# Opening attention with q ahead of k and cosine products on GpSimd, and sending routing logits to all partitions through DRAM

## The chip, the cores and the metric

One core of one Trainium2 chip runs the whole program. The metric is the device time of one execution in microseconds (us). Five engines work side by side, each on its own queue of instructions: TensorE (PE), VectorE (DVE), ScalarE (ACT), GpSimd (POOL) and SyncE (SP, which issues DMAs here; ACT and POOL issue some too).

## The reference

Attention, then two mixtures of experts on its output. Cut to what is computed:

```python
q_rot, k_rot = rotate(q), rotate(k)               # B=2, H=8, S=576, D=64; cos and sin of position
attn = softmax(q_rot @ k_rot.T / sqrt(D)) @ v     # 16 heads
x = attn.transpose(0, 2, 1, 3).reshape(1152, 512)
# first mixture: 8 experts on all tokens, weighted by a Sinkhorn-normalised gate
x = sum(P[:, e:e+1] * (relu(x @ w1[e]) @ w2[e]) for e in range(8))
# second mixture: greedy routing with a capacity of 144 tokens per expert
for idx in argsort(-(x @ w_gate).flatten()):
    tok, e = idx // 8, idx % 8
    if assigned[tok] < 0 and counts[e] < 144:
        assigned[tok] = e; counts[e] += 1
out[assigned == e] = relu(x[assigned == e] @ w1[e]) @ w2[e]
```

## The kernel before, in words

**Opening.** The 16 heads are worked as 8 pairs. Pair 0 has nothing to hide behind, so `attention` writes its first steps out by hand. k of head 0 is loaded first on SP, q of head 0 and the table of cosines and sines (`tcs`) on ACT (L1276 to L1281). The function `first` (L1328) rotates one head on DVE: two products with the sine (L1334, L1335) into a scratch tile `t`, the product with the cosine in place (L1337), and their sum into `t1k` or `t1q` (L1338). It is called for k of head 0, q of head 0 and k of head 1. ACT writes q a second time beside itself (`twice`, L1343). PE transposes both (`tq`, L1382), ACT and DVE copy the transposes out of PSUM as `qk` (L1398, L1400), and PE makes the scores `S` (`sc`, L1415), of which DVE takes the maximum (`mx`, L1424) and ACT the exponential (`ex`, L1429). q of head 1 and all later heads are rotated on GpSimd (`rot`, L1323 to L1326) from wider tables `tabk` and `tabq`, which ACT makes from `tcs`. `warm` (L1375) issues matmuls whose result nobody reads; their numbers are in `WARM`. The order of the steps of one pair is the string `ORDER`; pair 0 follows `FIRST`, the same string with the three steps of head 1's transposes (`tq1 qb1 qa1`) moved behind `te1 pb0 ex2`.

**Routing of the second mixture.** The function `moe2` assigns tokens in 8 phases, one expert filled in each. Phase p takes every token's best logit `m` among the experts still open (`prefer`, L205 and L206), spreads all 1152 values of `m` to all 128 partitions as `mb`, compares them with each partition's own nine (DVE: `compare`, L245 to L248; ACT for the first part of tables j = 5 to 8: `above`, L237 and L239), counts by 81 small matmuls how many tokens stand ahead (`count`, L256), assigns and closes an expert. From that come the token indices (`place`, `spread`, `index`, `address`), two indirect DMAs on GpSimd that gather the tokens (`gather`, L360: `xa`, `xb`), and eight DMAs of 512 KB on SP with the expert's weights (`weights`, L380 and L384). The expert itself is 64 matmuls on 144 tokens (L471, L481) with transposes in and out. Phase 0's `mb`, and that of all others before the change, is made by nine transposes of a broadcast column on PE (`bcast`, L213) and three copies on ACT (`bcopy`, L216).

The order of all this is fixed when the program is built. The class `Plan` holds each step with what it depends on and its booked times, one (engine, duration, latency) for each engine it passes, and always takes the step that can start first. The experts' matmuls are a main line in their own order; routing steps are put between them where the books say that their operands are there:

```python
op(f"bc{c}", ["m"], [("PE", 0.33, 0.2)], bcast, c)
op(f"mb{c}", [f"bc{c}"], [("ACT", 0.37, 0.1)], bcopy, c)
op("wlo", ["sel" if last else "close"] + ...,
   [("SP", 0.3, 0), ("DMA", 7.0 if p else 3.5, 2.0)], weights, 0, 4 if p else 2)
```

`wlo` and `whi` are the two halves of an expert's weight loads. `HOLD` names phases in which DVE waits for the gather of the phase before (`hold`, L335) ahead of compare j.

## Time and profile before

| | |
|---|---|
| time, median of 3 runs | 1123.04 us (1122.49 to 1125.29) |
| the profiled execution's own time | 1122.86 us |
| its span | 1121.1 us, 20946 instructions |
| mean granted clock of TensorE | 0.996 of full speed |
| busy share of the span | PE 98%, DVE 67%, POOL 39%, ACT 37% |
| chain that ended last, by engine | PE 88%, DVE 3%, DMA 3%, issue 2%, ACT 2%, POOL 1% |

The span is what the profiler recorded on the core; the 1.76 us that the execution took beyond it lie before the first and behind the last recorded instruction. The chain of waits is followed back from the last instruction to what released it, so its shares tell on which engine time would have to be saved. In a timeline, each row has its start and its duration in us, the engine, the program line, the operation with output and inputs, and in brackets the idle time before it and what ended that.

### The profile page before, as it was taken

What the parts mean: (1) busy time and instruction counts of PE and PEld (TensorE: products, weight loads), DVE (VectorE), ACT (ScalarE), POOL (GpSimd) and SP (SyncE); (2) the same over time, 40 slices, a digit from 0 to 9 for tenths busy, and PEclk for the clock granted to TensorE, in tenths of its full rate; (3) what the DMA queues carried; (4) which work ended last, traced back from release to release, by engine and by line L of the source; (5) the groups of instructions that cost most, each with busy time, mean ns of one, the idle gap of its engine ahead of it and who ended that gap; (6) DMA issues with size and microseconds to landing.
All of it is one profiled execution on the core that took longest, in us unless ns stands there. A gap on an engine that the chain in (4) does not pass through costs nothing.

```text
span 1121.1 us, 20946 instructions
## 1 busy us (share of the span) xinstructions
PE 1102.6 (98%) x8171; PEld 962.0 (86%) x8171; DVE 745.7 (67%) x1688; ACT 412.8 (37%) x903; POOL 438.6 (39%) x449
## 2 busy tenths in 40 slices
PE   7999999999999999999999999999999999999997
PEld 4666678998888888888888889989889888999997
DVE  5777733564777777777777777666678887778200
ACT  5777742143223223222223223232331133566222
POOL 6778353065434335434334534345310000234211
PEclk8999999999999999999999999999999999999999
DMA  5332322001233222432322422112130004879920
GB/s 130 79 74 51 99 82 76 1 1 57 82 98 94 85 86 88 125 98 75 95 85 75 126 92 66 38 39 74 39 141 11 30 1 165 277 250 354 292 75 22
DMA packets 105458, 107.22 MB, mean 96 GB/s; under 512 B 35600, under 2 KB 68752, under 8 KB 105232
## 3 DMA queue, kind: packets, MB, share of 16 engines
q1 hardware_dynamic: 102528, 100.40, 28.6%
q0 software_dynamic: 2048, 4.72, 1.4%
q8 instruction: 64, 1.05, 0.4%
q10 hardware_dynamic: 784, 0.77, 0.2%
q14 instruction: 34, 0.28, 0.1%
HBM read 98.85 MB, written 4.72 MB: 92 GB/s over the span
## 4 chain that ended last, share of the span: by engine, by line
PE 88%; DVE 3%; DMA 3%; issue 2%; ACT 2%; POOL 1%; SPq 1%; POOLq 0%; DVEq 0%; ACTq 0%
PE Y L1001 23%; PE T L939 21%; PE T L750 9%; PE Y L769 8%; PE Y L471 5%; PE Y L481 5%; PE T L1454 3%; PE S L1415 3%; PE T L1382 3%; DMA fr<-in_moe_w 2%; PE T L256 1%; DVE acc L1003 1%; PE PV L1382 1%; DVE v L952 1%; PE PV L1454 1%
## 5 line engine op out<-in xcount | busy, mean ns | idle before, releaser
L939 PE MATMUL T<-xH,wa 128*128 128x256 f32 (+1 forms) x576 | 137.8, 294 | 0.9 <-ACT v L959 0.8
L939 PEld LDWEIGHTS T<-big,wb 128*128 128x128 f32 x864 | 125.7, 188 | 10.8 <-DVE v L952 1.8
L939 PE MATMUL T<-big,wb 128*128 128x256 f32 (+1 forms) x864 | 133.0, 296 | 0.0
L952 DVE TENSOR_TENSOR v<-T,v 128x256 f32<-128x256 f32 (+1 forms) x240 | 108.1, 450 | 37.4 <-PE T L939 34.5
L1003 DVE SCALAR_TENSOR_TENSOR acc<-Y,pw,acc 128x512 f32<-128x512 f32 x168 | 122.5, 742 | 1.5 <-PE Y L1001 0.4
L939 PEld LDWEIGHTS T<-xH,wa 128*128 128x128 f32 x576 | 100.0, 188 | 9.5 <-ACT v L959 3.8
L750 PE MATMUL T<-xH,wa 128*128 128x384 f32 x336 | 92.9, 337 | 0.0
L848 POOL TENSOR_TENSOR wa<-wraw,wa 128x512 fp32r<-128x512 f32 (+1 forms) x48 | 48.8, 1018 | 106.3 <-ACT wa L847 106.3
L945 ACT ACTIVATE hhA<-v 128x256 fp32r<-128x256 f32 x72 | 30.1, 418 | 149.3 <-DVE v L952 149.3
L939 PE MATMUL T<-xL,wa 128*128 128x256 f32 (+1 forms) x288 | 84.5, 293 | 0.0
L945 ACT ACTIVATE hhB<-v 128x320 fp32r<-128x320 f32 x72 | 34.0, 472 | 136.5 <-DVE v L952 136.5
L946 DVE SCALAR_TENSOR_TENSOR hlB<-v,hhB 128x320 fp32r<-128x320 f32 x72 | 57.0, 792 | 38.7 <-ACT hhB L945 38.7
L1001 PE MATMUL Y<-wa,hhB 128*128 128x512 f32 x240 | 75.2, 395 | 0.0
L1001 PE MATMUL Y<-wb,hhB 128*128 128x512 f32 x240 | 75.2, 395 | 0.0
L1073 DVE SCALAR_TENSOR_TENSOR fr<-fr,fc 128x512 f32<-128x512 f32 x64 | 52.5, 820 | 33.6 <-DMA fr<-in_moe_w 33.6
L946 DVE SCALAR_TENSOR_TENSOR hlA<-v,hhA 128x256 fp32r<-128x256 f32 x72 | 51.1, 709 | 35.3 <-ACT hhA L945 35.3
L867 POOL TENSOR_TENSOR wb<-wraw,wb 128x512 fp32r<-128x512 f32 x24 | 30.6, 1299 | 101.9 <-ACT wb L866 101.9
L867 POOL TENSOR_TENSOR wa<-wraw,wa 128x512 fp32r<-128x512 f32 x24 | 30.6, 1294 | 99.1 <-ACT wa L866 99.1
L769 PE MATMUL Y<-wb,hh 128*128 128x512 f32 x216 | 68.4, 398 | 0.0
L750 PEld LDWEIGHTS T<-xH,wa 128*128 128x128 f32 x336 | 61.3, 188 | 2.9 <-issue 0.9
L1424 DVE TENSOR_REDUCE negmax<-S 128x1 f32<-128x576 f32 x72 | 53.8, 748 | 15.0 <-PE S L1415 14.1
L1001 PE MATMUL Y<-wa,hhA 128*128 128x512 f32 x192 | 59.9, 393 | 0.0
(343 smaller groups left out, 2729.1 us busy)
## 6 DMA issues: line engine op xcount, KB each, us to landing
wraw<-in_moe_w SPq DMA_DIRECT2D x52, 512.0 KB, 5.4
fr<-in_moe_w SPq DMA_DIRECT2D x64, 256.0 KB, 5.1
wraw<-in_moe_w SPq DMA_DIRECT2D x48, 256.0 KB, 3.2
big<-in_moe_w SPq DMA_DIRECT2D x20, 512.0 KB, 7.9
wa<-in_moe_w SPq DMA_DIRECT2D x18, 512.0 KB, 5.2
wb<-in_moe_w SPq DMA_DIRECT2D x14, 512.0 KB, 7.6
fc<-in_moe_w_gate SPq DMA_DIRECT2D x9, 256.0 KB, 3.5
t1q<-t1q SPq DMA_DIRECT2D x14, 160.0 KB, 2.8
```

The lines of the kernel that those rows point to most:

```text
L471: nc.tensor.matmul(Z["ph"][:, f % 2], d["wa"][kt // 2][:, kt % 2, f * 128:(f + 1) * 128], Z["xg", p][:, kt], start=(kt == 0), stop=(kt == ...
L481: nc.tensor.matmul(Z["py"][:, b % 2], d["wb"][f // 4][:, f % 4, b * 128:(b + 1) * 128], Z["h", p][:, f], start=(f == 0), stop=(f == FB - 1))
L750: nc.tensor.matmul(p[:, :CH], w[:, wi, kt, (fb % 2) * 128:(fb % 2) * 128 + 128], x[:, kt, o], start=(n == 0), stop=(n == 11))
L769: nc.tensor.matmul(self.Y[c][t], a[:, o], w[:, wi, fb % 2], start=(fb == 0 and n == 0), stop=(fb == FB - 1 and n == 2))
L867: G.tensor_tensor(d["W"][:, 1, h], r[:, 2 + h], d["W"][:, 0, h].bitcast(F32), op=OP.subtract)
L939: nc.tensor.matmul(bank[:, 0:n], d[t][:, ww, b, r * 128:(r + 1) * 128], x(xw, r), start=(first and i == 0), stop=(i == 5), skip_group_chec ...
L945: A.activation(HH[:, f, o], src, AF.Relu)
L946: V.scalar_tensor_tensor(HL[:, f, o], src, 0.0, HH[:, f, o].bitcast(F32), op0=OP.max, op1=OP.subtract)
L952: V.tensor_tensor(o, bank[:, 0:n], x, op=OP.add)
L1001: nc.tensor.matmul(y, h[:, f, o], w[:, ww, f], start=(f == 0 and z == 0), stop=(f == 1 and z == 2))
L1003: V.scalar_tensor_tensor(self.at(t), y, self.pw[:, t, e:e + 1], self.at(t), op0=OP.mult, op1=OP.add)
L1424: V.tensor_reduce(m[0:n], SS[P, i][0:n, :, :288], axis=AX.XY, op=OP.max, negate=True)
```

## The change

**Opening.** q of head 0 is loaded first on SP and its part of the table first on ACT; k of head 0 goes to ACT's queue. The memsets of q and of the warm matmuls' operand come first on GpSimd. `first` is split in three: `first_cos` makes the cosine product on GpSimd straight into `t1q` or `t1k`, `first_sin` the two sine products on DVE, `first_add` the sum on DVE. q of head 0 comes ahead of k of head 0. ACT makes only the table of q ahead; that of k, the sine products of k of head 1, two warm matmuls, and the rotations of pair 1 are issued behind head 0's transposes (`begin`), four warm matmuls behind the second scores, and k of head 1's sum behind the second maximum. The `qk` copies of head 0 are made in two pieces each. The first warm matmuls are 9 in place of 14. Head 1's transposes stay where they were, their copies come later.

**Routing.** For phases 1 to 6, `m` is transposed once (to 9 partitions of 128), copied by ACT, written to DRAM by a DMA on ACT's queue, and read back by one DMA on SP's queue that gives all 1152 values to each partition. The books give the write 2.2 us and the read 3.4. The first half of the weights of experts 1 to 5 is issued behind the read of the next phase. The hold of phase 1 stands one compare earlier.

```diff
@@ -90,7 +90,7 @@
         m1.dbg = dbg["acc"]
         nc.sync.dma_start(dbg["lg"], lg)
     xst.close()
-    moe2(tc, nc, ctx, ps, m1, w1b, w2b, ident, lg, ysc, out)
+    moe2(tc, nc, ctx, ps, m1, w1b, w2b, ident, lg, ysc, dram, out)
 
 
 TINY = 2.0 ** -120
@@ -164,11 +164,11 @@
 
 
 CFG = dict(CG=3, NCMP=6, HA=20, LEAD=8, FILL=0)
-JA = 5
-MAIN, HOLD, AT = 0.715, {1: 1, 2: 0}, (33, 34)
-
-
-def moe2(tc, nc, ctx, ps, m1, w1b, w2b, ident, lg, ysc, out):
+JA, VIA = 5, 1
+MAIN, HOLD, AT = 0.715, {1: 0, 2: 0}, (33, 34)
+
+
+def moe2(tc, nc, ctx, ps, m1, w1b, w2b, ident, lg, ysc, dram, out):
     BIG = 3.0e38
     FAR = 1.0e6
     if True:
@@ -206,6 +206,20 @@
                 V.tensor_reduce(m, lm, axis=AX.X, op=OP.max)
                 d["lm"], d["m"] = lm, m
                 d["mb"] = two.tile([128, NT, 128], F32, name="mb")
+
+            def turn_m():
+                pt = ps.tile([128, 512], F32, name="PV", bufs=1)[0:NT, 0:128]
+                nc.tensor.transpose(pt, d["m"], ident)
+                d["mt"] = two.tile([NT, 128], F32, name="mt")
+                nc.scalar.activation(d["mt"], pt, AF.Copy)
+
+            def send_m():
+                d["mr"] = dram.tile([NT, 128], F32, name=f"mr{p}")
+                nc.scalar.dma_start(d["mr"], d["mt"])
+
+            def spread_m():
+                nc.sync.dma_start(d["mb"].rearrange("p t c -> p (t c)"),
+                                  d["mr"].rearrange("t c -> (t c)").partition_broadcast(128))
 
             def bcast(c):
                 d["pm", c] = pm = ps.tile([128, 512], F32, name="T", bufs=3)[:, 0:384].rearrange("p (t c) -> p t c", t=3)
@@ -391,9 +405,17 @@
 
             if not last:
                 op("m", [("close", p - 1), ("left", p - 1)] + ([("at", p)] if p == 1 else []) if p else [("fold", 1)], [("DVE", 0.5, 0.15)], prefer)
-                for c in range(3):
-                    op(f"bc{c}", ["m"], [("PE", 0.33, 0.2)], bcast, c)
-                    op(f"mb{c}", [f"bc{c}"], [("ACT", 0.37, 0.1)], bcopy, c)
+                if p < VIA:
+                    for c in range(3):
+                        op(f"bc{c}", ["m"], [("PE", 0.33, 0.2)], bcast, c)
+                        op(f"mb{c}", [f"bc{c}"], [("ACT", 0.37, 0.1)], bcopy, c)
+                else:
+                    op("ms", ["m"], [("PE", 0.12, 0.2), ("ACT", 0.25, 0.1)], turn_m)
+                    op("mw", ["ms"], [("ACT", 0.06, 0.0)], send_m)
+                    op("ml", ["mw"], [("NONE", 0.0, 2.2)], lambda: None)
+                    op("mi", ["ml"], [("SP", 0.1, 0.0)], spread_m)
+                    for c in range(3):
+                        op(f"mb{c}", ["mi"], [("NONE", 0.0, 3.4)], lambda: None)
                 op("oh", ["m"] + ([("ad", p - 1)] if p in HOLD else []), [("DVE", 1.35, 0.1)], onehot)
                 mb = ["mb0", "mb1", "mb2"]
                 for j in range(JA, NT):
@@ -415,7 +437,7 @@
                 op("sel", ["close", "left"], [("DVE", 0.6, 0.1)], select)
             else:
                 op("sel", [("sel", p - 1), ("left", p - 1)], [("DVE", 1.3, 0.1)], select)
-            op("wlo", ["sel" if last else "close"] + ([("yend", p - 3)] if p > 2 else []) + ([("whi", p - 1)] if p else []) + ([("t", 35)] if p == 1 else []),
+            op("wlo", ["sel" if last else "close"] + ([("yend", p - 3)] if p > 2 else []) + ([("whi", p - 1)] if p else []) + ([("t", 35)] if p == 1 else []) + ([("mi", p + 1)] if max(VIA - 1, 1) <= p < E - 2 else []),
                [("SP", 0.3, 0), ("DMA", 7.0 if p else 3.5, 2.0)], weights, 0, 4 if p else 2)
             op("pl", ["sel"], [("PE", 0.2, 0.2)], place)
             op("spr", ["pl"], [("DVE", 1.65, 0.1)], spread)
@@ -1273,24 +1295,24 @@
 
         tcs = pone.tile([128, 11, 64], F32, name="tcs")
         wb = one.tile([128, 512], BF, name="wb")
-        load_k(nc.sync, 0, (0,), False)
+        load_q(nc.sync, 0, (0,), False)
+        A.dma_start(tcs[:, 0:5], rope[:, 0:5])
+        nc.sync.dma_start(*load_tail("q", 0))
+        load_k(A, 0, (0,), False)
+        nc.sync.dma_start(tcs[:, 5:11], rope[:, 5:11])
         nc.sync.dma_start(*load_tail("k", 0))
-        A.dma_start(tcs[:, 5:11], rope[:, 5:11])
-        load_q(A, 0, (0,), False)
-        A.dma_start(*load_tail("q", 0))
-        A.dma_start(tcs[:, 0:5], rope[:, 0:5])
+        G.memset(raw["q", 0][64:128, :, 4, :], 0.0)
+        G.memset(wb, 0.0)
         G.memset(raw["k", 0][32:64, :, 4:6, :], 0.0)
         G.memset(raw["k", 0][64:128, :, 4:6, :], 0.0)
-        G.memset(raw["q", 0][64:128, :, 4, :], 0.0)
-        G.memset(wb, 0.0)
         for t in vs:
             G.memset(t[64:128, 4], 0.0)
         G.memset(raw["k", 1][:, :, 4:6, :], 0.0)
         G.memset(raw["q", 1][64:128, :, 4, :], 0.0)
+        load_q(nc.sync, 0, (1,), False)
+        nc.sync.dma_start(*load_tail("q", 1))
         load_k(nc.sync, 0, (1,), False)
         nc.sync.dma_start(*load_tail("k", 1))
-        load_q(nc.sync, 0, (1,), False)
-        nc.sync.dma_start(*load_tail("q", 1))
         load_q(nc.sync, 1, (0, 1))
         load_k(nc.sync, 1, (0, 1))
         load_v(0)
@@ -1300,7 +1322,9 @@
             V.memset(t, 1.0)
         for i in range(NE):
             V.memset(eb[i][:, 576:640], 0.0)
-        for n, o in (("k", slice(5, 11)), ("q", slice(0, 5))):
+
+        def tables(n):
+            o = slice(0, 5) if n == "q" else slice(5, 11)
             A.activation(tab[n][:, :, 64:96], tcs[:, o, 32:64], AF.Copy, scale=-1.0)
             A.activation(tab[n][:, :, 96:128], tcs[:, o, 32:64], AF.Copy)
             A.activation(tab[n][:, :, 0:64].rearrange("p j (u c) -> p j u c", u=2),
@@ -1325,17 +1349,27 @@
             e.tensor_tensor(x[:, o], x[:, o], table(0, 64), op=OP.mult)
             e.tensor_tensor(T1[n, P][:, o, :, 0], x[:, o], t, op=OP.add)
 
-        def first(n, h, z):
-            x, J = raw[n, 0][:, h], SL[n]
+        def first_cos(n, h):
+            J = SL[n]
             if h == 0:
                 T1[n, 0] = ptwo.tile([128, 2, J, 2 if n == "q" else 1, HD], F32, name="t1" + n)
-            t = t2[:, z, :J]
+            c = tcs[:, 0:5] if n == "q" else tcs[:, 5:11]
+            G.tensor_tensor(T1[n, 0][:, h, :, 0].rearrange("p j (u c) -> p j u c", u=2),
+                            raw[n, 0][:, h].rearrange("p j (u c) -> p j u c", u=2),
+                            c[:, :, 0:32].unsqueeze(2).to_broadcast([128, J, 2, 32]), op=OP.mult)
+
+        tv = [t2[:, 0], t2[:, 1], None]
+
+        def first_sin(n, h, z):
+            x, J = raw[n, 0][:, h], SL[n]
+            t = tv[z][:, :J]
             c = tcs[:, 0:5] if n == "q" else tcs[:, 5:11]
             V.scalar_tensor_tensor(t[:, :, 0:32], x[:, :, 32:64], -1.0, c[:, :, 32:64], op0=OP.mult, op1=OP.mult)
             V.tensor_tensor(t[:, :, 32:64], x[:, :, 0:32], c[:, :, 32:64], op=OP.mult)
-            x2 = x.rearrange("p j (u c) -> p j u c", u=2)
-            V.tensor_tensor(x2, x2, c[:, :, 0:32].unsqueeze(2).to_broadcast([128, J, 2, 32]), op=OP.mult)
-            V.tensor_tensor(T1[n, 0][:, h, :, 0], x, t, op=OP.add)
+
+        def first_add(n, h, z):
+            x = T1[n, 0][:, h, :, 0]
+            V.tensor_tensor(x, x, tv[z][:, :SL[n]], op=OP.add)
 
         def twice(P, h, act=False):
             t = T1["q", P]
@@ -1394,7 +1428,11 @@
                 QK[P, h] = two.tile([128, 1024], F32, name="qk", bufs=QB)
             d = QK[P, h].rearrange("p (s a c) -> p s a c", a=2, c=64)
             x = bank[hold["q", P, h][r]]
-            if r == 0:
+            f = V.tensor_copy if r else lambda d, x: A.activation(d, x, AF.Copy)
+            if (P, h) == (0, 0):
+                for lo, hi in ((0, 5), (5, 8 - r)):
+                    f(d[:, lo:hi, r], x[:, lo * 64:hi * 64].rearrange("p (s c) -> p s c", c=64))
+            elif r == 0:
                 A.activation(d[:, 0:8, 0], x.rearrange("p (s c) -> p s c", c=64), AF.Copy)
             else:
                 V.tensor_copy(d[:, 0:7, 1], x[:, 0:448].rearrange("p (s c) -> p s c", c=64))
@@ -1512,16 +1550,30 @@
                    rbc=rbc, ra=ra, rb=rb, nm=nm, xs=xs, rk=lambda P: rk(P + 2), rq=lambda P: rq(P + 2),
                    lv=lambda P: load_v(P) if P > 1 else None)
 
-        first("k", 0, 0)
-        first("q", 0, 1)
+        tv[2] = two.tile([128, 576], F32, name="rs")[:, 0:384].rearrange("p (j d) -> p j d", d=HD)
+        tables("q")
+        first_cos("q", 0)
+        first_sin("q", 0, 1)
+        first_add("q", 0, 1)
         twice(0, 0, True)
-        first("k", 1, 0)
-        rot(0, "q", (1,), G, 0)
+        first_cos("k", 0)
+        first_sin("k", 0, 0)
+        first_add("k", 0, 0)
+        rot(0, "q", (1,), G, 1)
+        first_cos("k", 1)
         load_q(nc.sync, 2, (0, 1))
-        load_k(nc.sync, 2, (0, 1))
-        rq(1)
-        rk(1)
+
+        def begin():
+            tables("k")
+            first_sin("k", 1, 2)
+            warm(2)
+            load_k(nc.sync, 2, (0, 1))
+            rq(1)
+            rk(1)
+
         warm(WARM[0])
+        AHEAD = {"qa0>": begin, "sc1": lambda: warm(WARM[2]),
+                 "mx1": lambda: first_add("k", 1, 2)}
         for p in range(-1, NP + 3):
             if p == NP and m1:
                 own = [0]
@@ -1535,6 +1587,8 @@
                 if f == "tq1" and P == 0:
                     twice(0, 1, True)
                 run[x](P, *(int(c) for c in f[len(x):]))
+                if w in AHEAD:
+                    AHEAD.pop(w)()
                 if x == "te" and P == 0:
                     warm(WARM[1])
                 if f == "tq1" and P == NP - 1:
@@ -1546,13 +1600,14 @@
                         getattr(m1, g[0])(*g[1:])
 
 
-WARM = (14, 2)
+WARM = (9, 2, 4)
 NC, QB = 9, 3
 ORDER = """sc0 te7< mx0 sc1 pa7< pb7< te8< ex0 pv01<< mx1 pa8< pb8< ex1 tq1 nm0<< lv sc2 qb1 qa1 te0 mx2 sc3 pa0
 te1 pb0 ex2 pv10< den< mx3 rcp< xs<< pa1 pb1 ex3 rbc< sc4 rb< ra< te2 mx4 sc5 pa2 pb2 ex4 rq te3 mx5 pv11< pa3 pb3
 ex5 sc6 nm1< te4 mx6 rk tq0> pa4 sc7 pb4 ex6 qb0> te5 sc8 qa0> mx7 pa5 te6 pb5 ex7 pv00< mx8 pa6 pb6 ex8"""
 MOVED = "tq1 qb1 qa1"
-FIRST = " ".join(x for x in ORDER.split() if x not in MOVED.split()).replace("te1 pb0 ex2", "te1 pb0 ex2 " + MOVED)
+FIRST = " ".join(x for x in ORDER.split() if x not in MOVED.split()).replace("te1 pb0 ex2", "te1 pb0 ex2 tq1")
+FIRST = FIRST.replace("pa1 pb1 ex3", "pa1 pb1 qa1 qb1 ex3")
 AFTER = {("pb3", 0): (("wconv", 0, 0, True),), ("pb5", 0): (("wconv", 0, 1, True), ("wload", 2)),
          ("pa8", 1): (("wconv", 1, 0),), ("rcp", 1): (("step",), ("wconv", 1, 1), ("gate_w",), ("wload", 3))}
```

The places where the order of instructions moves most are these. On DVE, in the opening, the rows of `first` before the change (`rawk_97` and `rawq_95` are k and q of pair 0, `t_101` the scratch tile; k's four rows come once more behind these, for head 1, ahead of the first copy):

```order
L1334 SCALAR_TENSOR_TENSOR t_101<-rawk_97,tcs 128x6x32
L1335 TENSOR_TENSOR t_101<-rawk_97,tcs 128x6x32
L1337 TENSOR_TENSOR rawk_97<-rawk_97,tcs 128x384
L1338 TENSOR_TENSOR t1k<-rawk_97,t_101 128x384
L1334 SCALAR_TENSOR_TENSOR t_101<-rawq_95,tcs 128x5x32
L1335 TENSOR_TENSOR t_101<-rawq_95,tcs 128x5x32
L1337 TENSOR_TENSOR rawq_95<-rawq_95,tcs 128x320
L1338 TENSOR_TENSOR t1q<-rawq_95,t_101 128x5x64
```

And the same place on DVE with the change, as far as the first two maxima and the sum behind them:

```order
L1367 SCALAR_TENSOR_TENSOR t_101<-rawq_95,tcs 128x5x32
L1368 TENSOR_TENSOR t_101<-rawq_95,tcs 128x5x32
L1372 TENSOR_TENSOR t1q<-t1q,t_101 128x5x64
L1367 SCALAR_TENSOR_TENSOR t_101<-rawk_97,tcs 128x6x32
L1368 TENSOR_TENSOR t_101<-rawk_97,tcs 128x6x32
L1372 TENSOR_TENSOR t1k<-t1k,t_101 128x384
L1434 COPY qk<-T 128x5x64
L1434 COPY qk<-T 128x2x64
L1367 SCALAR_TENSOR_TENSOR rs<-rawk_97,tcs 128x6x32
L1368 TENSOR_TENSOR rs<-rawk_97,tcs 128x6x32
L1462 TENSOR_REDUCE negmax<-S 128x1 x2
L1372 TENSOR_TENSOR t1k<-t1k,rs 128x384
```

The cosine products have left DVE, q stands ahead of k, and the sine products of k's second head have moved from ahead of the copies to between the copies and the maxima.

On GpSimd with the change, the rows behind its memsets (before it, L1323 to L1326 for q of head 1 stood there first, `tabq` being q's wide table):

```order
L1357 TENSOR_TENSOR t1q<-rawq_95,tcs 128x5x64
L1357 TENSOR_TENSOR t1k<-rawk_97,tcs 128x384
L1347 TENSOR_TENSOR t_101<-rawq_95,tabq 128x5x32
L1348 TENSOR_TENSOR t_101<-rawq_95,tabq 128x5x32
L1349 TENSOR_TENSOR rawq_95<-rawq_95,tabq 128x320
L1350 TENSOR_TENSOR t1q<-rawq_95,t_101 128x5x64
```

Two cosine products have come ahead of the rotation of q's second head; a third, of k's second head, follows it, and then come the rotations of pair 1 as before.

On ACT in the last broadcast phase, with the semaphores that each row waits for; before the change (`oa` and `ob` are an expert's output, `h` its hidden layer, `cmp` a table of compares):

```order
L491 ACTIVATE oa<-Y 72x512 [waits DMASW4_49,PE_49]
L216 ACTIVATE mb<-T 128x384 [waits PE_49]
L491 ACTIVATE ob<-Y 72x512 [waits DMASW5_49,PE_49]
L216 ACTIVATE mb<-T 128x384
L216 ACTIVATE mb<-T 128x384 [waits PE_49]
L237 ACTIVATE cmp_11608<-mb,m 128x640 [waits DVE_49,Activation_49]
L474 ACTIVATE h<-Y 128x288 [waits PE_49]
```

With the change:

```order
L214 ACTIVATE mt<-PV 9x128 [waits DMAHW7_49,PE_49]
L496 ACTIVATE h<-Y 128x288 [waits PE_49]
L218 DMA mr_11658<-mt 9x128 [waits DMAHW3_49,Activation_49]
L496 ACTIVATE h<-Y 128x288 [waits PE_49] x2
L251 ACTIVATE cmp_11739<-mb,m 128x640 [waits DMAHW4_49,DVE_49]
L251 ACTIVATE cmp_11747<-mb,m 128x768
```

The three copies are one of 9 x 128 and the issue of the write; three copies of `h` now stand between the transposed `m` and the first compare, which waits for a DMA in place of ACT's own copies.

## Rows read from the trace of the kernel before

**Rows 1.** The page: the head, and the chain that ended last by engine.

```profile
span 1121.1 us, 20946 instructions
...
PE 88%; DVE 3%; DMA 3%; issue 2%; ACT 2%; POOL 1%; SPq 1%; POOLq 0%; DVEq 0%; ACTq 0%
```

**Rows 2.** The chain of waits in the opening (start us, us, what).

```profile
11.05 0.77 PE S L1415 x4
11.84 0.77 DVE negmax L1424
...
13.52 1.33 PE S L1415 x4
...
20.85 0.76 PE S L1415 x4
...
21.91 0.54 PE T L1375 x2
```

**Rows 3.** The timeline of the opening, DVE, POOL and PE.

```profile
5.32 0.36 DVE L1334 SCALAR_TENSOR_TENSOR t<-rawk,tcs 128x192 f32<-128x192 f32 x1 [3.94 <-DMA rawk<-in_k]
...
7.63 0.49 DVE L1337 TENSOR_TENSOR rawq<-rawq,tcs 128x320 f32<-128x320 f32 x1
...
11.68 0.86 POOL L1325 TENSOR_TENSOR rawq<-rawq,tabq 128x320 f32<-128x320 f32 x1
...
22.45 1.82 POOL L1326 TENSOR_TENSOR t1k<-rawk,t 128x768 f32<-128x768 f32 x1
...
25.80 0.35 PE L1382 MATMUL T<-ident,t1k 64*128 64x64 f32 x5
```

**Rows 4.** Windows: PE, PEld, DVE, ACT, POOL busy (count), granted clock, DMA share, GB/s.

```profile
12.00:13.00 1.00, 0.29 (x4) 0.00 (x0) 1.00 (x2) 0.36 (x1) 0.92 (x2) 1.00 0.83 190
13.00:14.00 1.00, 0.48 (x2) 0.48 (x4) 0.26 (x1) 1.00 (x4) 0.92 (x2) 0.53 0.61 140
...
19.00:20.00 1.00, 1.00 (x16) 0.91 (x15) 0.00 (x0) 0.00 (x0) 1.00 (x2) 0.56 0.35 77
```

**Rows 5.** The timeline in the first mixture, DVE and POOL.

```profile
337.17 0.43 DVE L946 SCALAR_TENSOR_TENSOR hlA<-v,hhA 128x256 fp32r<-128x256 f32 x1 [0.48 <-ACT hhA L945]
...
338.93 1.86 POOL L848 TENSOR_TENSOR wb<-S,wb 128x768 fp32r<-128x768 f32 x1
...
339.72 1.35 DVE L946 SCALAR_TENSOR_TENSOR hlA<-v,hhA 128x256 fp32r<-128x256 f32 x1 [0.48 <-ACT hhA L945]
```

**Rows 6.** PE's waits from 925 to 1120 (total, times, longest); three rows alike.

```profile
PE Y L490 <- ACT y L484: 0.3, 1, 0.3
```

**Rows 7.** The timeline of routing phase 4 and the start of 5.

```profile
990.50 0.23 DVE L206 TENSOR_REDUCE m<-lm 128x9 f32<-128x72 f32 x1
...
991.41 1.15 PE L213 MATMUL T<-ident,m 128*128 128x128 f32 x9
...
994.12 0.74 DVE L247 TENSOR_SCALAR cmp<-mb,m 128x1024 bf16<-128x1024 f32 x1
...
1006.60 0.23 DVE L206 TENSOR_REDUCE m<-lm 128x9 f32<-128x72 f32 x1
```

**Rows 8.** DMA issues of the whole span (KB each, median us to landing).

```profile
fc<-in_moe_w_gate SPq DMA_DIRECT2D x9, 256.0 KB, 3.5
...
g<-in_moe_w_gate SPq DMA_DIRECT2D x1, 2048.0 KB, 7.5
...
ysc<-acl SPq DMA_DIRECT2D x1, 256.0 KB, 2.0
ysc<-acl ACTq DMA_DIRECT2D x1, 256.0 KB, 5.5
```

**Rows 9.** A window of the routing, columns as in rows 4.

```profile
1004.00:1024.00 20.00, 20.00 (x260) 19.85 (x259) 16.54 (x66) 11.75 (x20) 3.75 (x7) 1.00 1.03 343
```

**Rows 10.** The chain of waits in two experts of the routing's end.

```profile
1047.48 6.13 PE Y L471 x50
...
1064.64 6.13 PE Y L471 x50
```

## The prediction

> **What bounds the kernel now.** I read the page first: a span of 1121.1 us and a chain of waits that is 88% TensorE (PE) [rows 1]. So a change gains only where it takes work off PE, takes a wait of PE away, or lets PE run faster; elsewhere the question is whether PE still finds its operands in time. The change touches two stretches, the first 25 us and the 130 us of routing from 935 on, so I read the chain and the timeline of the first, then PE's waits and the timeline of the second.
>
> In the opening the chain passes through loads, DVE and ACT; the first score matmuls stand at 11.05, the first maximum at 11.84, and from 20.85 on one score step follows another on PE (1.60 us, 20.85 to 22.45), with warm matmuls filling the gaps [rows 2]. The windows show a second cost: PE was busy for 0.29 and 0.48 of two windows, the granted clock fell to half in the second of them, and it was full again only in the window after 20 [rows 4]. That is TensorE's lower level, 1.2 GHz in place of 2.4.
>
> In the routing, PE is the bound without a gap: three waits of 0.2 to 0.3 us in 190 us [rows 6]. The order there is written at build time from booked durations, so an operation that comes later than booked stops PE at the matmul that needs it.
>
> **The change, the opening.** The sum is made against the profiled execution, 1122.86 us (1121.1 and 1.76 around it), 0.18 below the median of 1123.04.
>
> Now DVE does four operations on k, then four on q. Sine of k began at 5.32 [rows 3]. With q first on SP and its table first on ACT, I estimate q at about 4.5 (k needed three transfers on SP, q needs two), and k, now on ACT's queue and SP's fourth, at about 5.6. The cosine product moves from DVE (0.49 us for 320 columns) to GpSimd, where a product of that shape takes 0.86 us; for k's 384 columns that makes 1.03 [rows 3].
>
> If the two engines worked side by side, k's sum would be ready at 7.2 or so and the scores at 8.2 in place of 11.05. I don't believe that, because of one pair of rows: the same DVE instruction, two operands in SBUF, takes 0.43 us alone and 1.35 us when a GpSimd instruction of 1.86 us is under way, and it ends when that one ends (338.93 + 1.86 = 340.79; 339.72 + 1.35 = 341.07) [rows 5]. So I lay the operations one after another: q's sine pair 0.6 (0.36 each, overlapping) and cosine 0.86 from 4.5, q's add 6.0 to 6.5, ACT's doubling to 7.0, q's transposes behind it; k's sine pair to 7.1, k's cosine to 8.1, k's add to 8.7 (up to 9.1 where GpSimd's next operation holds it), transposes 0.35, copies 0.6: scores at 9.4 to 10.4. The first maximum gains less. In DVE's queue it now stands behind the sine pair of k's second head, and that meets GpSimd's rotation of q's second head (four operations, one of them the 0.86). I get 11.3 to 11.9 against 11.84, so 0 to 0.6.
>
> The rest has to come from the clock. From 13.52 to 20.85 PE takes 7.33 us for two score steps and one set of head 1's transposes; at the full clock two steps of 1.60 and some 1.3 for the transposes and their copies make 4.5, which is 2.8 less [rows 2]. The change puts two warm matmuls between the transposes and the scores and four (1.1 us by the 0.54 for two) behind the second scores, where PE now idles (12.29 to 13.52, the window's 0.29 and the next score [rows 2, 4]). PE then works almost without a gap over the stretch in which the clock fell. I take **-2.8** for clock and earlier start together. Lower end -4.3: GpSimd's queue ends pair 1's rotation at 24.27, PE needs it at 25.80 [rows 3], and the three cosine products (2.9 us) go into that queue; started at 5.6 without a delay the queue ends at 21.4, so PE could come forward by 25.80 - 21.4 = 4.4 at most. Upper end 0: the clock falls as before and the locks eat the rest. Once the scores run PE bounds (20.85 on), so what is gained stays.
>
> Work that costs nothing: both orders have the same PE instructions; ACT's k table comes later but only pair 1's rotation needs it; the warm matmuls dropped ahead (14 to 9) covered a wait.
>
> **The change, the routing.** Six phases lose nine broadcast transposes and three copies and get one transpose, one copy and two transfers. The nine took PE from 991.41 to 992.39, 0.98 us; one of nine stays, 0.11 [rows 7]. 6 x 0.87 = **-5.2**, all on PE's path, as PE has no gap to absorb it. That is the lower end.
>
> Against it stands the way through DRAM. The code books 2.2 us for the write, 0.1 for the issue and 3.4 for the broadcast, 5.76 with ACT's issue; PE's fixed order puts the count matmuls where the compares are done by that book. From rows: a write of 256 KB to DRAM landed in 2.0 us from SP's queue, and one of the same size from ACT's queue, with the DMA engines full, in 5.5 [rows 8]; this one is smaller (4.5 KB) and on ACT's queue. The broadcast has two neighbours of its kind, from one place in DRAM to all partitions: 256 KB in 3.5, 2048 KB in 7.5. Straight between them, 576 KB takes 3.5 + 320/1792 x 4.0 = 4.2. The lighter rows are nearer, because the SP order puts the broadcast ahead of the next expert's 2 MB of weights, and the weights of the one before have mostly landed by then. So write 2.0, broadcast 4.2: 6.2 in place of 5.76, 0.4 late.
>
> Who waits for it: on DVE the nine compares, on ACT the Sign operations of tables 5 to 8, with the y and xg copies queued behind them, and behind both the count matmuls that stand next on PE. The loop shows that lateness isn't absorbed: from the first compare to the next phase's m it took 12.5 us (994.12 to 1006.60) [rows 7], with about 2 from m to the write and 6.2 for the way makes 20.6, while PE has 17.16 us of expert (1047.48 to 1064.64 [rows 10]) and the count, index and place matmuls per phase. The two are near each other, and PE's order is fixed, so a late broadcast becomes a wait of PE: 6 x 0.4 = **+2.4**. Net **-2.8**.
>
> The Trainium skill (SBUF — State Buffer, "The DMA setup-cost knee") gives a fixed 2 us and 436 GB/s, an estimate of 3.4 us for this broadcast where the rows between which it lies say 4.2. By that page nothing would be late, the routing would give -5.2 and the whole 1114.9; the 256 KB broadcast at 3.5 (the fit would give 2.6) speaks against it, so I go by the rows.
>
> Edits that cost nothing by themselves: weights of expert p now wait behind the broadcast, 3 to 4 us later than the earliest, under an expert of 17.16 us; the broadcast adds 576 KB to a stretch in which the DMA share is already 1.03 [rows 9], some 1.7 us of 20 at 340 GB/s, hidden as long as weights land before their expert. DVE's hold for the gather comes one compare earlier in phase 1 only, where DVE waits for mb anyway.
>
> **Sum.** 1122.86 - 2.8 - 2.8 = 1117.3. A measurement of this kernel can tell 0.3%, 3.4 us, from no change.
>
> **Rivals.**
> A: *everything hides*, chance 0.18. GpSimd and DVE hardly meet, or the write and broadcast make 5.8 together. Routing -5.2 with the opening between -2.8 and -4.3: 1114.9 to 1113.4. For it: the 2.0 us write. Against: rows 5 and the 256 KB broadcast.
> B: *one half gives nothing*, chance 0.27. The clock falls anyway (opening 0, total 1120.1), or the way takes 6.6 (5.2 / 6 = 0.87 late, routing 0, total 1120.1), or both (1122.9). For it: one gap in front of the maximum is enough to lose the clock, as before. That the changed order doesn't reach the start of the scores at all, since DVE and GpSimd only swap places, belongs here.
> C: *the way through DRAM becomes the bound*, slower, chance 0.12. In a stretch with the DMA engines full the write and the broadcast queue behind weights and gather packets. With the opening's 2.8 the sum is over 3.4 slower from a way of 5.76 + (5.2 + 2.8 + 3.4) / 6 = 7.7 us; at 8.5 it is 6 x 2.74 - 5.2 - 2.8 = +8.4, 1131.3. For it: the 5.5 us write on ACT's queue and share 1.03. Against: the share counts mostly weights, and the order sends them behind the broadcast.
> The forecast keeps 0.43.
>
> **Range.** From 1112.8 (just under A) to 1124.5 (B in full and the beginning of C) leaves out about 0.15. Faster by over 0.3% (under 1119.7): forecast and A, 0.61. Within: B, 0.27. Slower: C, 0.12.
>
> **What would show it.** In the profile after: first scores near 10 and the first maximum near 11.6; DVE's sine and add rows 0.3 to 0.8 longer than 0.35 and 0.56 where a GpSimd row ends with them; PEclk full from 12 to 20, the step at 20.85 near 18. In the routing: one transpose of 9 x 128 per phase, a write of 2.0, a broadcast of 4.2, and six waits of PE on compares (or the ACT copies behind them) of about 0.4. A clock at half between 13 and 19 makes B right; a broadcast row of 6 us or more, with waits of PE of 2 us per phase, makes C right; a broadcast of 3.4 and no waits makes A right. If the routing takes longer with a short broadcast, my reading of the fixed order is wrong.

## The result, and the profile after

| | before | with the change |
|---|---|---|
| median, 22 runs each | 1122.39 us (1120.04 to 1126.23) | 1129.40 us (1123.21 to 1137.84) |
| ratio to before | | 1.0064 (95%: 1.0050 to 1.0078) |
| profiled execution, span | 1121.1 us | 1128.6 us |
| its mean granted clock | 0.996 | 0.992 |

The change is slower by 0.64%, some 7 us, where 1117.3 was predicted and 1124.5 was the end of the range. The times of single runs spread over 14.6 us, and they go with the granted clock: the three fastest runs (1123.2 to 1123.7) had 0.996 or 0.997, the three slowest (1135.6 to 1137.8) 0.986 or 0.987. A straight line through the 22 runs gives 11.6 us for each hundredth of the clock, and 1124.4 at 0.996, the mean clock of the profile before. So, as an estimate from these runs, some 2 of the 7 us are there at the old clock, and 5 come with the lower one.

The page of the changed kernel, the head and the chain that ended last by engine, against [rows 1]:

```profile
span 1128.6 us, 20870 instructions
...
PE 88%; DMA 5%; issue 3%; POOL 1%; DVE 1%; SPq 1%; ACT 0%; POOLq 0%; DVEq 0%; ACTq 0%
```

The DMA share of the chain rose from 3% to 5%, and the line under it names one transfer for most of that, the gather `xb<-ysc,ix` with 4%. TensorE's (PE's) waits in the routing, against [rows 6] (total us, times, longest):

```profile
PE Y L468 <- DMA xb<-ysc,ix: 6.5, 6, 2.4
PE Y L477 <- DMA xa<-ysc,ix: 2.2, 1, 2.2
PE T L270 <- DVE cmp L262: 0.5, 1, 0.5
PE Y L512 <- ACT y L506: 0.3, 1, 0.3
```

Before, PE waited 0.7 us there; now 9.5, of which 8.7 are waits for gathered tokens (L477 for expert 0, L468 for the others) and 0.5 for the compares that the forecast looked at. The windows around the first two of these waits, columns as in [rows 4]:

```profile
940.00:944.00 4.00, 1.79 (x8) 1.13 (x6) 1.41 (x5) 1.27 (x2) 1.91 (x3) 1.00 0.83 266
944.00:948.00 4.00, 3.98 (x46) 3.89 (x47) 4.00 (x12) 4.00 (x6) 0.00 (x0) 0.80 0.87 281
948.00:952.00 4.00, 3.94 (x52) 3.11 (x50) 2.68 (x9) 2.29 (x4) 0.00 (x0) 0.78 1.03 375
968.00:972.00 4.00, 2.55 (x17) 2.35 (x15) 2.25 (x9) 2.70 (x4) 0.00 (x0) 0.78 1.04 323
972.00:976.00 4.00, 4.00 (x48) 3.90 (x47) 0.00 (x0) 1.76 (x4) 0.00 (x0) 0.50 1.05 385
976.00:980.00 4.00, 4.00 (x44) 3.70 (x42) 1.83 (x10) 0.60 (x2) 1.40 (x4) 0.50 0.16 58
980.00:984.00 4.00, 4.00 (x39) 3.91 (x38) 2.87 (x13) 1.48 (x4) 0.94 (x1) 0.94 0.26 74
```

PE idles in part of the first and of the fourth window, and behind each the granted clock is lower while PE has work. Adding (1 - clock) x 4 over the six windows behind the first gives 6.8 us, about 6.5 without the idle part of the fourth: an estimate of what the lower clock cost in this profile.

So the routing's account closes. From the first m (917.40 before, 914.52 after) to the span's end it took 203.7 us before and 214.1 after, 10.4 more. The forecast's -5.2 for the transposes, 8.8 more of waits and 6.5 of clock make +10.1.

One phase in the timeline, phase 4 of the changed kernel with the gather of expert 3, shows where the way through DRAM stood and where the wait came:

```profile
1004.59 0.23 DVE L206 TENSOR_REDUCE m<-lm 128x9 f32<-128x72 f32 x1
...
1005.39 0.27 PE L212 MATMUL PV<-ident,m 128*9 128x128 f32 x1
...
1006.25 0.27 ACTq L218 DMA_DIRECT2D mr<-mt  x1
...
1007.54 0.34 SPq L221 DMA_DIRECT2D mb<-mr  x1
1009.01 0.98 POOL L374 DMA_INDIRECT xa<-ysc,ix  x1 [3.85 <-PE Y L493]
1010.30 0.97 POOL L374 DMA_INDIRECT xb<-ysc,ix  x1 [0.30 <-PE Y L493]
1011.23 0.75 DVE L261 TENSOR_SCALAR cmp<-mb,m 128x1024 bf16<-128x1024 f32 x1 [3.05 <-DMA mb<-mr]
...
1018.65 0.28 PE L468 MATMUL Y<-ident,xb 72*128 72x72 f32 x1 [0.92 <-DMA xb<-ysc,ix]
```

From the issue of the write to the first compare it is 4.98 us: the broadcast could be issued 1.3 us behind the write, and the compare started 3.7 us behind the broadcast (the DMA rows have the landing of four of the six broadcasts, 3.5 to 4.3 us). The book said 5.76, so nothing was late in this phase. The other ways were 9.0 (phase 1), 5.2, 7.5 (phase 3), 5.2 and 4.9: two of six were late, by 3.2 and 1.7 us, and yet PE's waits on compares come to 0.5 us in all. Here the second gather, issued at 1010.30, had landed only at 1018.6, and PE already stood at the transposes of its tokens. The DMA rows from 945 to 1105, before and after, say that a gather took 0.3 and 1.1 us longer than before (the last number is the median from issue to landing):

```profile
xa<-ysc,ix POOLq DMA_INDIRECT x7, 7.1
xb<-ysc,ix POOLq DMA_INDIRECT x7, 7.3
```

```profile
xa<-ysc,ix POOLq DMA_INDIRECT x7, 7.4
xb<-ysc,ix POOLq DMA_INDIRECT x7, 8.4
```

What differs is when it is needed. Before, expert 3's second gather was issued at 996.33 and its tokens were transposed only at 1018.08:

```profile
996.33 5.68 POOL L360 DMA_INDIRECT xb<-ysc,ix  x1 [0.31 <-PE Y L481]
...
1018.08 0.23 PE L445 MATMUL Y<-ident,xa 72*128 72x72 f32 x1
```

That is 21.8 us; after the change, 8.4. From an expert's second gather to its first transposed token it was 10.7 us at expert 1 before and 21.8 to 31.6 at experts 3 to 6; after the change it is 6.2 to 8.1 at each of experts 1 to 6, and a gather takes 7.4 to 8.4 (the medians above). Phases stood 16 to 20 us apart before, while the experts' first transposes stood up to 23.6 apart (17.16 where no routing is between them [rows 10]), so routing gained on the experts. After the change phases stand 21 to 25 apart (m at 1004.59 and 1026.24, for one) and the experts 21 to 27: the lead no longer grows.

Expert 0's wait, the first in the windows above, has a part of the new way in it. These are phase 1's rows:

```profile
933.76 0.55 ACTq L218 DMA_DIRECT2D mr<-mt  x1
...
938.43 0.34 SPq L221 DMA_DIRECT2D mb<-mr  x1
938.86 0.38 SPq L1061 DMA_DIRECT2D ysc<-acl  x1
...
939.71 1.15 POOL L374 DMA_INDIRECT xa<-ysc,ix  x1 [10.56 <-issue]
...
942.73 0.75 DVE L261 TENSOR_SCALAR cmp<-mb,m 128x1024 bf16<-128x1024 f32 x1 [0.35 <-DMA mb<-mr]
```

SP stood at the broadcast until the write had landed, 4.7 us. Behind it in SP's order is the last store of tokens (`ysc<-acl`), whose operand was ready at 937.71, so it went out 1.15 us late, and the gather of expert 0 follows 0.85 us behind that store. Before the change, and in the runs that leave phase 1 on transposes, the store goes out within 0.04 us of its operand. So, by this estimate, about 1 of the 2.2 us waited for expert 0 is the way's own.

### The profile page after: what moved, and what is told of

It is laid out like the page before. It is cut to its first block, busy times and chain, and to the rows that moved or that the text cites. A ratio compares the mean times of both kernels' runs of the same rounds, so it can differ in the third digit from the quotient of the medians.

```text
span 1128.6 us, 20870 instructions
## 1 busy us (share of the span) xinstructions
PE 1104.2 (98%) x8121; PEld 961.5 (85%) x8124; DVE 748.7 (66%) x1686; ACT 408.5 (36%) x892; POOL 429.3 (38%) x452
## 4 chain that ended last, share of the span: by engine, by line
PE 88%; DMA 5%; issue 3%; POOL 1%; DVE 1%; SPq 1%; ACT 0%; POOLq 0%; DVEq 0%; ACTq 0%
PE Y L1023 27%; PE T L961 24%; PE T L772 9%; PE Y L791 8%; DMA xb<-ysc,ix 4%; PE Y L493 4%; PE T L1492 3%; PE S L1453 3%; PE T L1416 2%; PE Y L503 2%; PE T L270 1%; PE PV L1416 1%; PE PV L1492 1%; PE Y L512 1%; PE PV L1125 1%
## 6 DMA issues: line engine op xcount, KB each, us to landing
wb<-in_moe_w SPq DMA_DIRECT2D x14, 512.0 KB, 11.9
```

## The experiments

Theory G says that the loss comes from gathers that PE reaches before they have landed, because the longer loop of a phase used up the lead of routing over the experts, and from the clock's falls behind those waits. Rival D says that the way through DRAM costs its own time in each phase. All ratios are to runs of the kernel before on the same chip.

**The opening alone.** The change with `JA, VIA = 5, 8` and the hold of before.

> Opening of the change, routing as before it. In the profile of the change the second mixture's first m stands at 914.5 in place of 917.4, and TensorE's clock no longer falls in the first 20 us. If that is the opening's whole effect, this is 2.9 us faster than before: about 1119.5. If the earlier start is given back later (the first mixture is not bound by TensorE alone), it is within 1 us of before, 1121.5 to 1123.

Measured: 1120.74 us, 0.9984 (0.9972 to 0.9995), by this ratio 1.8 us faster than before, between the two expectations. The opening's gain is there, smaller than its 2.8 or 2.9.

**The routing alone.** The kernel before with the change's edits to `moe2`.

> Opening as before, routing of the change. If the two halves are independent, this is 2.9 us slower than the change: about 1132 in the median, spread as widely as the change's runs (1126 to 1141), with TensorE waiting some 9 us on gathers. If the opening's new order had part in the loss, it is no slower than 1128.

Measured: 1129.15 us, 1.0063 (1.0041 to 1.0084), between the two expectations, with 7.6 us of waits on gathers. That is 7.1 slower than before; with the opening's -1.8 it is 5.3, against 7.2 (5.6 to 8.8) for the whole, so within what the intervals allow the halves add up, and the loss is the routing's.

**Three phases through DRAM in place of six.**

```diff
-JA, VIA = 5, 1
-MAIN, HOLD, AT = 0.715, {1: 0, 2: 0}, (33, 34)
+JA, VIA = 5, 4
+MAIN, HOLD, AT = 0.715, {1: 1, 2: 0}, (33, 34)
```

> The change with the way through DRAM in phases 4 to 6 alone (phases 1 to 3 keep the transposes; hold as before). Theory G, the loss comes from gathers that TensorE reaches before they have landed, because the longer loop of every phase ate the lead that routing had over the experts: with three phases the lead suffices, TensorE waits on no gather, three phases save 0.87 each, and with the opening it is 1122.4 - 2.9 - 2.6 = 1116.9. Theory D, each phase through DRAM costs its own time (the way of 5.3 us is longer than what it replaces): half of the routing's loss stays, 1122.4 - 2.9 + 5 = 1124.5.

Measured: 1117.41 us, 0.9952 (0.9934 to 0.9971). PE's waits in this run:

```profile
PE Y L512 <- ACT y L506: 0.3, 1, 0.3
PE Y L477 <- DMA xb<-ysc,ix: 0.2, 1, 0.2
```

Three phases use the same way, and no wait belongs to it: D falls, at least for these phases. From the second gather to the first transpose it is still 14 to 18 us for experts 4 to 6. The time from the first m to the end is 201.1 us, 2.6 less than before, as three times 0.87.

**An honest book for the gather.** The change with all six phases; only what the planner believes of the gathers of experts 1 to 7 is changed, and so the places of their transposes in PE's order.

```diff
             op("la", ["ga"], ...)
+            op("lt", ["ga"], [("NONE", 0.0, 7.0)], lambda: None)
...
-                op(f"tin{h}", ["la"] + ...
+                op(f"tin{h}", ["lt"] + ...
```

> The change, but the book says that a gather has landed 7.0 us after its issue instead of 4.0 (for the transposes of the gathered tokens only), so TensorE's fixed order has more work between the index and those transposes. Theory G: the 9.5 us of waits fall under 3 and the clock has less reason to fall: 1115 to 1119. Theory D: TensorE waits elsewhere, on compares, and the time stays between 1125 and 1132.

Measured: 1120.67 us, 0.9984 (0.9970 to 0.9999), 8.7 us under the change's median (9.0 by the ratios). PE's waits in this run:

```profile
PE Y L478 <- DMA xa<-ysc,ix: 2.2, 1, 2.2
PE T L270 <- DVE cmp L262: 1.1, 3, 0.6
...
PE Y L469 <- DMA xb<-ysc,ix: 0.3, 1, 0.3
```

The six waits on `xb` shrank from 6.5 to 0.3 us by a reordering alone. The 2.2 us of expert 0, which this edit doesn't touch, stayed, and the clock fell behind it once more (0.50 from 948 to 952). Theory G holds in its main part; the time is 1.7 above the end of its range, less than that wait and the fall together cost. The change's earlier hold in phase 1 is in this run too, and no run tests it by itself.

**Holding back the second half of the weights.** SP reads a word of the gathered `xb` ahead of an expert's second 2 MB, so it issues them once the gather has landed.

```diff
-                elif p < 4:
+                elif p == 0:
                     nc.sync.value_load(tick[0:1, 0:1], min_val=0, max_val=1)
                 else:
-                    nc.sync.value_load(d["ix"][0:1, 0:1], min_val=0, max_val=N)
+                    nc.sync.value_load(d["xb"][0:1, 0:1].bitcast(I32), min_val=-2**31, max_val=2**31 - 1)
```

> The change with one wait more: SP issues the second half of each expert's weights (2 MB) when that expert's gather has landed, not when it has been issued. Theory G1, the gather is late because it shares the DMA engines with 4 MB of weights: a gather lands in 5 to 6 us in place of 7.4 to 9.2, TensorE's waits on gathers fall from 9 us to under 3, and the time to 1118 to 1122. Theory G2, the gather takes no longer than before the change (6.5 to 8) and only its place in TensorE's order is too early: the waits stay at 6 us or more and the time between 1125 and 1132.

Measured: 1128.84 us, 1.0049 (1.0034 to 1.0064). The gathers landed in 6.1 and 7.9 us (medians of the same stretch, 7.4 and 8.4 in the change); PE still waited 5.6 us for them, a little under G2's 6, and 1.8 at the transpose of m. The time is G2's. Without the traffic of those 2 MB a gather takes 1.3 and 0.5 us less, which is not enough to end the waits.

**Weights ahead of the broadcast.** The change without `("mi", p + 1)` among what `wlo` waits for.

> The change without its rule that an expert's first weights go behind the next phase's broadcast. The broadcast then queues behind 2 MB on SP and lands in 8 to 10 us in place of 3.9, booked at 3.4. This is the slower case as I had priced it: each us beyond the book costs 1 us per phase, so 6 x 5 = 30 us at most, 1140 to 1160, with TensorE waiting on compares. If the planner's order puts the broadcast ahead anyway, nothing moves (1125 to 1132).

Measured: 1162.74 us, 1.0380 (1.0348 to 1.0411). PE's waits, and one phase's write and broadcast on the queues:

```profile
PE T L270 <- DVE cmp L262: 16.7, 15, 3.3
PE Y L477 <- DMA xa<-ysc,ix: 3.0, 1, 3.0
PE Y L468 <- DMA xb<-ysc,ix: 2.4, 1, 2.4
PE PV L212 <- DVE pos L340: 2.0, 4, 0.6
```

```profile
1041.98 0.27 ACTq L218 DMA_DIRECT2D mr<-mt  x1
1046.89 0.34 SPq L221 DMA_DIRECT2D mb<-mr  x1
...
1052.72 0.75 DVE L261 TENSOR_SCALAR cmp<-mb,m 128x1024 bf16<-128x1024 f32 x1 [8.65 <-DMA mb<-mr]
```

Here the way takes 10.7 us in place of 5.0, and the waits are on compares. Both halves of it grew, the write of 4.5 KB from 1.3 to 4.9 us, too, though it is on another queue than the weights; the broadcast took 4.8 to 7.4 us from its issue to the first compare in phases 2 to 6, not the 8 to 10 expected. This is the slower rival's mechanism, with a time 2.7 us above its range, and it shows that in most phases the change's order of weights and broadcast keeps it away.

**Work in place of the waits.** PE gets matmuls on data at hand, with results that nobody reads, ahead of the transposes of gathered tokens.

```diff
+            def idle(pt, n):
+                for _ in range(n):
+                    nc.tensor.matmul(pt..., ones_b, d["hot"]...[:, 0:2 * CAP], start=True, stop=True, ...)
...
+                if h == 0:
+                    idle(pt, 10)
...
+                if h == 0:
+                    idle(Z["pt"][0], 18)
```

> The change with matmuls that nobody reads ahead of the transposes of the gathered tokens (18 of 128 x 288 in bf16 for expert 0, 10 for each other, 0.12 us each), so that TensorE works where it waited for gathers. They add 2.2 + 7 x 1.2 = 10.6 us of work against 9 us of waits. Theory K, the clock's fall behind a wait is a cost of its own (6 us in the profile of the change, and what makes its runs differ by 14 us): the clock stays, runs lie close together and the median falls to 1124 to 1126. If the clock's falls have another cause, the time is 1129 to 1132, as widely spread as before.

Measured: 1129.78 us (1126.20 to 1133.23, 4 runs), 1.0069 (1.0045 to 1.0094). The expected gain didn't come. Two waits on `xb`, 2.2 us together, were left, so 10.6 us of added work had replaced only some 6.5 of waits. The clock did stay up: 0.996 to 0.998 in its four timed runs, where the change's 22 had 0.986 to 0.997, and in the routing of its profile only 1080 to 1088 fell, behind the longer of those waits (1.9 us). Its windows where the change had lost its clock first:

```profile
944.00:948.00 4.00, 4.00 (x34) 3.45 (x33) 4.00 (x11) 4.00 (x6) 0.00 (x0) 1.00 0.70 233
948.00:952.00 4.00, 3.94 (x71) 3.38 (x70) 3.72 (x13) 3.25 (x5) 0.00 (x0) 1.00 0.96 330
```

With the idle time gone, the falls there are gone; that avoiding them pays isn't shown, as the filling cost what it saved.

**Two and three phases back on transposes, with the honest book.** `VIA` is 2 in the first and 3 in the second, with the hold of before and the edit of the book above.

> The way through DRAM in phases 2 to 6, the hold as before, and a gather booked as landed 7.0 us after its issue. In the run that booked 7.0 with phases 1 to 6, what was left was a wait of 2.2 us near 941 in phase 1 and the clock's fall behind it (944 to 956). Theory G: with phase 1 back on transposes both go, five phases save 0.87 each: opening -1.6, routing -4.4, so 1122.2 - 6.0 = 1116.2. Theory D: the loop of the phases through DRAM is longer than an expert, so waits of 1 to 2 us per phase appear on compares or gathers: 1120 to 1124.

Measured: 1118.84 us, 0.9966 (0.9954 to 0.9979): faster, not as far as 1116.2. PE still waited 0.9 us for expert 0's gather, and the clock fell behind it (0.50 from 948 to 956).

> The way through DRAM in phases 3 to 6, the hold as before, a gather booked at 7.0 us. Against the run with phases 4 to 6 one phase more saves 0.87 on TensorE. Theory G, the lead of routing over the experts pays for the way: with the lead not yet used up in phase 3 and the honest book, no wait comes back and the time is 1116.0 to 1117.5. Theory D: the time is above that of phases 4 to 6 (1117.4) by more than 1 us.

Measured: 1120.82 us, 0.9991 (0.9982 to 1.0000), over the bound that it was to keep. PE waited twice 1.07 us at the transpose of m for `pos` on DVE: that transpose and the matmuls that make the input of `pos` (L340) use the same PSUM bank, `PV`, of which there is one.

**Three runs on one chip.** The first repeats `VIA = 4`; the second is `VIA = 3` without the edit of the book; the third books expert 0's gather at 4.3 in place of 2.1 as well, with all six phases.

> Phases 4 to 6 through DRAM once more, on the chip of the next two. Theory G: 0.995 of before again, 1116.5 to 1118. If the first result was luck of few runs, it is 1119 to 1121, where the opening alone stands.

> Phases 3 to 6 through DRAM, the gather booked at 4.0 as in the change. In the run with the honest book TensorE waited twice 1.07 us at the transpose of m for DVE, which had still to read another result from the same PSUM bank. If the book moved the steps into that wait, it is gone here and the time is that of phases 4 to 6 or up to 0.9 below it (1116 to 1118). If the fourth phase as such costs time, it is 1119 or above.

> The change in all six phases, with honest books for every gather: 7.0 us for those of experts 1 to 7, 4.3 in place of 2.1 for that of expert 0, whose late landing made the wait of 2.2 us near 941 and the clock's fall behind it. Theory G: no wait over 1 us, no fall of the clock, 1122.2 - 1.8 - 5.2 + 1 = 1116.2, up to 1118. Theory D: 1120 or above, with new waits on compares or at the transpose of m.

Measured: 1118.69 us, 0.9959 (0.9944 to 0.9974) for `VIA = 4`; 1122.32 us, 0.9994 (0.9982 to 1.0007) for `VIA = 3`; 1120.85 us, 0.9970 (0.9949 to 0.9990) for the honest books. So the first result repeats. The fourth phase costs time with either book. It isn't the number of phases, though: five of them with the honest book were faster (0.9966) than four with it (0.9991). PE's waits with `VIA = 3`:

```profile
PE PV L212 <- DVE pos L340: 2.1, 2, 1.1
PE Y L493 <- issue: 1.7, 2, 1.0
...
PE T L270 <- DVE cmp L262: 0.2, 1, 0.2
```

The 2.1 at the transpose of m explain more than half of the difference to `VIA = 4`; the 1.7 ahead of an expert's first matmuls have no releaser in the trace and stay open. Both runs with `VIA = 3` have the two waits at the transpose of m, and the run with five phases has none there, so what these runs show against the fourth phase is the order that the planner made for it. The third run still waited 1.7 us for expert 0's gather, with the clock at 0.59 behind it (948 to 952), and 0.5 at the transpose of m in phase 3. Its median is in D's range; its ratio, on the 1122.2 from which its expectation was worked out, gives 1118.8, between the two. It leaves open how much of D is true.

**Cosine products back on DVE.** In the first version the product of k's second head stood behind the load that overwrites its input, so that it used k of pair 2 and waited for it; its time (1130.52 us) says nothing of the question.

> Opening of the change with the cosine products back on DVE (that of k's second head behind the second maximum), routing as before. In the profiles of the new opening GpSimd's rotations set the pace up to 34 us (k of pair 2 ends at 33.4 and TensorE goes on at 34.4), and GpSimd's three cosine products and DVE's rows lengthened beside them stand ahead of them. If GpSimd's queue is what limits the opening's gain, it runs 2 us earlier here and the time is 1.5 us below that of the opening alone (1120.7): 1119.2. If the scores' start limits it, DVE's three products more make it later: 1120.7 to 1122.

In the second that load was moved behind it.

```diff
-            G.tensor_tensor(T1[n, 0][:, h, :, 0]...
+            V.tensor_tensor(T1[n, 0][:, h, :, 0]...
...
-                 "mx1": lambda: first_add("k", 1, 2)}
+                 "mx1": lambda: (first_cos("k", 1), load_k(nc.sync, 2, (0, 1)), first_add("k", 1, 2))}
```

> Opening of the change with the cosine products on DVE, that of k's second head behind the second maximum and ahead of the load that overwrites its input (the load of pair 2's k moves behind it); routing as before. If GpSimd's queue is what limits the opening's gain, GpSimd's rotation of pair 2's k ends about 2 us before 33.4 and the time is 1.0 to 1.5 us below that of the opening alone (1120.7). If the scores' start limits it, DVE's products make the first maximum later than 11.6 and the time is 1120.7 to 1122.

Measured: 1122.43 us, 1.0001 (0.9988 to 1.0015). GpSimd was through with pair 1's k at 21.1 in place of 22.6, but then waited 2.4 us for k of pair 2, whose load the edit had made later, and ended that rotation at 34.3. On the question it is inconclusive: the edit moved the limit from the queue to the load. But it bears out what sets the pace further on. The sum of that rotation started 0.88 us later than in the run of the opening alone (32.46 for 31.58), and a maximum further on came 0.88 later, too (49.15 for 48.27).

**The best version** is the change with `VIA = 4`: 0.9952 and 0.9959 of before, 4.6 to 4.8 us faster than before and 11 to 12 faster than the change. The five phases with the honest book (0.9966, 0.9954 to 0.9979) can't be told from it.

## Why the prediction was wrong

**The opening, mechanism wrong, sign right.** The scores stood at 10.22 (forecast 9.4 to 10.4) and the first maximum at 11.60 (11.3 to 11.9). DVE's sine product beside GpSimd's cosine product took 1.15 us in place of 0.36, and ends within 0.25 us of it, as [rows 5] had it:

```profile
6.01 1.07 POOL L1357 TENSOR_TENSOR t1k<-rawk,tcs 128x384 f32<-128x384 f32 x1 [0.56 <-DMA rawk<-in_k]
6.14 1.15 DVE L1367 SCALAR_TENSOR_TENSOR t<-rawk,tcs 128x192 f32<-128x192 f32 x1
```

The Trainium skill (SBUF — State Buffer, "Who interferes with whom") states that a VectorE instruction with two SBUF inputs contends with a GpSimd instruction that reads SBUF, and calls the ports that they share an exclusive lock. These two rows agree, for VectorE's side.

The clock stayed full in this profile. But the -2.8 "for clock and earlier start together" was sized by what the clock gave back up to 20.85, and it did not carry. GpSimd's rotation of pair 2's k, with the copy `rcp` behind it in the same queue, sets the pace there. Its last row starts at 33.29 before, at 31.61 after, 1.68 earlier, and a maximum further on moves by as much, 49.98 to 48.30. With the change PE waits for that copy:

```profile
31.61 1.82 POOL L1350 TENSOR_TENSOR t1k<-rawk,t 128x768 f32<-128x768 f32 x1
...
34.44 0.46 PE L1416 MATMUL T<-ident,rcp 64*128 64x64 f32 x8 [0.22 <-POOL rcp L1504]
```

Before, PE came to the same place at 36.12, just as the copy ended (36.07). The run of the routing alone has the old opening, and in its profile that opening kept its clock. PE was there earlier, but waited 1.0 us for the copy, so that the two rows stand at 32.84 and 49.13, only 0.45 and 0.85 ahead of the profile that had lost its clock. Rows of DVE, before, routing alone and after:

```profile
49.98 0.76 DVE L1424 TENSOR_REDUCE negmax<-S 128x1 f32<-128x576 f32 x1
```

```profile
49.13 0.76 DVE L1446 TENSOR_REDUCE negmax<-S 128x1 f32<-128x576 f32 x1
```

```profile
48.30 0.76 DVE L1462 TENSOR_REDUCE negmax<-S 128x1 f32<-128x576 f32 x1
```

So the term is -1.7 by the profile and -1.8 (-3.1 to -0.6) by the runs. The first m of the routing came 2.9 earlier; the other 1.2 arose between 50 us and that m, and such a difference is not the opening's: in the profiles with the new opening and GpSimd's cosine products this maximum stands at 48.1 to 48.5 and the first m anywhere from 913.5 to 918.5. The forecast had GpSimd's queue as a bound for pair 1's k and didn't follow it to pair 2's, where it binds. The clock's fall in the opening is also no property of the old order: the old one has a profile without it (routing alone), and the new one has some with it (0.50 from 9 to 12 us in the run of the opening alone, where the maximum stands at 48.27 all the same).

**The transposes, -5.2: right in the account**, which closes within 0.3 us with it, though the transpose that is left has a row of 0.27 us and not 0.11. The two runs with three phases and no new wait bear it out: 2.6 and 2.3 us less from the first m to the end, for 3 x 0.87 = 2.6.

**The way through DRAM, +2.4: wrong.** This is the step "a late broadcast becomes a wait of PE: 6 x 0.4". The broadcast's price was close (4.2 for 3.5 to 4.3 where it has a landing); the write's was not (2.0 for 1.3 to 1.4 in five phases and 4.7 in phase 1). Four ways were 0.5 to 0.9 us earlier than their book and two were 3.2 and 1.7 late. That the mean, 6.1, is near the 6.2 of the forecast is luck. And the lateness didn't become waits of PE on compares: they came to 0.5 us, not 2.4. The Trainium skill (SBUF — State Buffer, "The DMA setup-cost knee") gave an estimate of 3.4 for the broadcast, within 0.1 of the fastest landing and 0.9 under the slowest; what followed from it, that nothing would be late, was so in four of six phases.

**What was costed at nothing.** The failing step is the loop: I found 20.6 us for a phase (the terms add up to 20.7; measured are 21.3 to 24.7) against an expert's 17.16 "and the count, index and place matmuls", and took from it only that a late broadcast isn't absorbed. It says something else first: a loop as long as PE's work for an expert and its routing ends the growth of routing's lead, and then every latency that the lead had covered is on PE's path. The gather (7 us before, too) was the next in line, with 6.45 in the planner's book from its first issue and 9.6 in the trace. Its cover had been named nowhere. In place of +2.4 came 8.8 of waits and 6.5 of clock. The honest book shows it for experts 1 to 7: with the gather booked at 7.0 their waits fell from 6.5 to 0.3.

**The clock in the routing** wasn't in the sum at all, although [rows 4] showed a fall behind a short idle time in the opening.

**Rival C** had the sign, a bound of the DMA side and a size (+8.4) near the measured +7, but at the wrong place. Its late way came in phases 1 and 3 only (9.0 and 7.5), with 0.5 us of waits on compares; in every phase it comes if the order of SP is turned round, which then costs 3.8%.

## What to carry to other kernels

A latency that costs nothing has a lead that pays for it: before a loop is made longer, list everything that this lead covers (here the gathers), with the time from issue to use, not only the new transfers. Look, too, at what stands behind a new transfer in its queue (here the store ahead of expert 0's gather). Where a planner's book fixes the order, its entries for latencies must be true once the slack is gone; a correction of one number brought 8.7 us. Take a longer way where there is a lead to spend: with the book as it was, three phases of six were faster than none or all; with the honest book, five came out alike.
